# One load of wo behind the last V instead of sixteen small ones, in a decode kernel for a gated attention and MLP mix

## The chip, the cores and the metric

The kernel runs on one core of one Trainium2 chip. A core has TensorE (PE, whose weight loads are listed as PEld), VectorE (DVE), ScalarE (ACT), GpSimd (POOL) and SyncE (SP), 16 DMA engines that are fed here by SP's queue, an SBUF of 128 partitions and a PSUM of eight banks. The metric is the time of one execution on the device in microseconds (us), as the median of several runs; smaller is better.

## The reference

```python
def reference(A_x, A_k_cache, A_v_cache, A_wq, A_wo, B_x, B_w1, ..., gate_w):
    # B=2, Sq=1, D=1024, H=32, Sk=16384, Dh=128, F=3584, all bf16
    x = A_x
    g = sigmoid((x * gate_w).sum(-1, keepdims=True))
    q = (x @ wq) -> [B, H, 1, Dh]
    p = softmax(q . k_cache * Dh**-0.5)           # over 16384 keys
    a = (p . v_cache) -> [B, 1, H*Dh] @ wo
    h  = gelu(layernorm(x) @ w1)
    hs = shifted quarters of h (all zero for one token) @ w2
    x1 = x + hs
    b  = x1 + gelu(layernorm(x1) @ w3) @ w4
    return g * a + (1 - g) * b
```

K and V are 268 MB each. All weights together are 36 MB, of them wo 8 MB (4096 rows of 1024) and w4 7 MB.

## The kernel before

**Units.** A unit is one batch row `b` and a pair of heads `hp` (16 pairs). Its K is 8 MB and its V is 8 MB: 128 partitions with 64 KB each. For a unit the kernel transposes K in eight chunks on DVE (line 423), multiplies each with the query on PE (429) into a PSUM tile S, takes the softmax (`softmax_a`, `softmax_b`), multiplies the weights with V on PE (`pv`, 483), and finishes in `pv_end`: ACT scales the sums (496), 16 matmuls gather the four lanes of the two heads (504), and DVE multiplies by the gate into `oT` (512), which holds one pair of heads for both batch rows. After the second batch row, `project` multiplies `oT` with the pair's 256 rows of wo and adds the result into the PSUM tile `arow` (375). `arow` holds the whole output, 4 groups of 256 columns on different partitions, in one bank; it starts with the residual of the MLP (`mlp_residual`), collects all 16 pairs, then w4's product (`mlp_last`, 403), and is copied out in four pieces by `write_out`, two on DVE (524) and two on ACT (526).

**Memory.** A large SBUF tile `mem` is cut into five cells of 32 KB a partition. K of batch row 0 takes cells 0 and 1, K of batch row 1 takes cells 1 and 2, V takes cells 3 and 4. The order of the chunks (`halves`) is such that cell 1, which both K's use, is read first. A transfer can start when the cells that it writes have been read: K's next load waits for DVE's transposes, V's next load for PE's `pv`. wo's 512 KB for a pair go to a tile of their own, `wo_pair`, in rows of 4 KB.

**Order.** The first unit's work stands ahead of a loop of 15 rounds over `hp`. A round is `odd_rest(hp)` and `even_unit(hp + 1)`. The last unit stands in an arm inside the loop (`tc.If(i >= HP - 2)`), which every engine jumps over in all rounds but the last. In the rounds without it, each engine instead counts up the semaphores that the arm would have counted. `in_order` keeps each engine's instructions in the order in which they are written, SP's too. SP issues in a round: wo (367), K of batch row 0 (112), V (115), K of batch row 1 (112), V (115). A load that waits holds back those written behind it. The built program lets wo's load wait until PE has come past the arm of the round before, since the arm's `project` reads `wo_pair`.

**The last arm.** It loads the last V into cells 0 and 1 (`V_LAST`), wo's last 512 KB, and, when `pv(0)` has read cells 3 and 4, all of w4 into these in four pieces of 15, 7, 4 and 2 rows a partition. Then come `pv(1)`, `pv_end(1)`, `project`, `mlp_last` piece by piece, and `write_out`.

Of the kernel before, what the change touches and what calls it, by code (L numbers as in the profile page):

```python
# [10 lines left out]
FP32 = mybir.dt.float32  # L11
BF16 = mybir.dt.bfloat16
ACTF = mybir.ActivationFunctionType
ALU = mybir.AluOpType
# [9 lines left out]
def kernel(  # L24
# [15 lines left out]
    nc = tc.nc  # L40
    P = nc.NUM_PARTITIONS
    B, Sq, D = A_x.shape
    _, H, Sk, Dh = A_k_cache.shape
# [3 lines left out]
    KC = D // P  # L47
    FC = F // P
# [4 lines left out]
    HALF = P // 2  # L53
    NJ = 2 * Sk // P
# [4 lines left out]
    Q4 = 4  # L59
    QP = P // Q4  # L60
    CELL = NJ * Dh // 2
    G1 = D // Q4
# [3 lines left out]
    const = ctx.enter_context(tc.tile_pool(name="const", bufs=1))  # L66
# [3 lines left out]
    mlp = ctx.enter_context(tc.tile_pool(name="mlp", bufs=1))  # L70
    ops = ctx.enter_context(tc.tile_pool(name="ops", bufs=1, space=PSUM))
# [8 lines left out]
    def region(cell, elements, offset=0):  # L80
        at = cell * CELL + offset
        return mem[:, at : at + elements]
# [6 lines left out]
    def load_weight(W, cell, offset=0, pieces=None):  # L89
        K, N = W.shape  # L90
        dst = region(cell, K // P * N, offset)
        src = W.rearrange("(p r) n -> p (r n)", p=P)
        r = 0
        for n in pieces or (K // P,):
            at = slice(r * N, (r + n) * N)
            nc.sync.dma_start(out=dst[:, at], in_=src[:, at])
            r += n
        return dst.rearrange("p (r n) -> p r n", n=N)
# [5 lines left out]
    K_CELL = (0, 1)  # L104
    V_CELL = 3

    def cache_rows(cache, hp, b):
        two = cache[b, bass.ds(2 * hp, 2)]
        return two.rearrange("h s d -> (h s) d").rearrange("(p j) d -> p (j d)", p=P)

    def load_k(hp, b):
        nc.sync.dma_start(out=region(K_CELL[b], NJ * Dh), in_=cache_rows(A_k_cache, hp, b))  # L112

    def load_v(hp, b, cell=V_CELL):
        nc.sync.dma_start(out=region(cell, NJ * Dh), in_=cache_rows(A_v_cache, hp, b))
# [6 lines left out]
        out=ident_s[:], in0=ident_f[:], scalar1=-scale, scalar2=None, op0=ALU.mult  # L122
# [7 lines left out]
    mask4 = const.tile([P, Q4], BF16)  # L130
    nc.gpsimd.memset(mask4[:], 1.0)
    nc.gpsimd.affine_select(
        out=mask4[:], in_=mask4[:], compare_op=ALU.is_ge, fill=0.0,
# [3 lines left out]
        out=mask4[:], in_=mask4[:], compare_op=ALU.is_ge, fill=0.0,  # L137
# [11 lines left out]
        out=lmat[:].rearrange("p (g h k) -> p g h k", h=2, k=4),  # L149
        in_=hm2[:].unsqueeze(1).unsqueeze(3).to_broadcast([P, P // 8, 2, 4]),  # L150
# [3 lines left out]
    lane = const.tile([P, QP], FP32)  # L154
    nc.vector.tensor_reduce(
        out=lane[:],
        in_=ident_f[:].rearrange("p (c k) -> p k c", k=QP),
        axis=AX.X,
        op=ALU.add,
# [3 lines left out]
    for g in range(Q4):  # L163
        nc.vector.tensor_scalar(
            out=spread[:, g],
            in0=lane[:].unsqueeze(1).to_broadcast([P, Q4, QP]),
            scalar1=mask4[:, g : g + 1], scalar2=None, op0=ALU.mult,
        )

    oacc = [ops.tile([P, 4 * Dh], FP32, name=f"oacc{k}") for k in range(2)]  # L170
    arow = ops.tile([P, G1], FP32, name="arow")
    S_tiles = [ops.tile([P, GT * QP], FP32, name=f"S{k}") for k in range(2)]
    for t in (oacc[0], oacc[1], arow):
        nc.vector.memset(t[:], 0.0)

    WW = P + NG
# [2 lines left out]
    for k in range(2):  # L179
        t = const.tile([P, 4, WW], BF16, name=f"qw{k}")  # L180
# [37 lines left out]
    g_rep = const.tile([P, B], FP32)  # L218
# [141 lines left out]
        )  # L360


    wo_pair = const.tile([P, 2, D], BF16, name="wo_pair")

    def load_wo(hp):
        rows = A_wo[bass.ds(hp * 2 * Dh, 2 * Dh)]
        nc.sync.dma_start(  # L367
            out=wo_pair[:].rearrange("p t n -> p (t n)"),
            in_=rows.rearrange("(p t) n -> p (t n)", p=P),
        )  # L370

    def project():
        for t in range(2):
            for g in range(Q4):
                nc.tensor.matmul(
                    arow[QP * g : QP * g + B, :],
                    lhsT=oT[:, t, :],
                    rhs=wo_pair[:, t, g * G1 : (g + 1) * G1],
                    start=False,
                    stop=False,  # L380
                    skip_group_check=True,
                )

    def mlp_residual():
        x1g = mlp.tile([P, KC, B], FP32, name="x1g")
        nc.vector.tensor_tensor(
            out=x1g[:], in0=x1T[:], in1=spread_batch(omg, KC), op=ALU.mult
        )
        for r in range(KC):
            for g in range(Q4):  # L390
                nc.tensor.matmul(
                    arow[QP * g : QP * g + B, :].rearrange("b (i r) -> b r i", r=KC)[:, r, :],
                    lhsT=x1g[:, r, :],
                    rhs=ident_f[:, QP * g : QP * (g + 1)],
                    start=(r == 0),
                    stop=False,
                    skip_group_check=True,
                )

    def mlp_last(w4):  # L400
        for r in range(FC):
            for g in range(Q4):
                nc.tensor.matmul(  # L403
                    arow[QP * g : QP * g + B, :],
                    lhsT=h2T[:, r, :],
                    rhs=w4[:, r, g * G1 : (g + 1) * G1],
                    start=False,
                    stop=(r == FC - 1),
                    skip_group_check=True,
                )  # L410

# [77 lines left out]
            )  # L489


    oT = const.tile([P, 2, B], BF16, name="oT")

    def pv_end(b):
        osb = ppool.tile([P, 4 * Dh], FP32, name="osb")
        nc.scalar.activation(  # L496
            out=osb[:], in_=oacc[b][:], func=ACTF.Copy, scale=rinvs[b][:, 0:1]
        )
        lines = osb[:].rearrange("p (k d t) -> p k t d", k=4, t=2)
        ot = misc_psum([P, 2])  # L500
        for t in range(2):
            for k in range(4):
                for h in range(2):
                    nc.tensor.matmul(  # L504
                        ot[h * HALF : (h + 1) * HALF, t : t + 1],
                        lhsT=lines[:, k, t, :],
                        rhs=lane[:, k + 4 * h : k + 4 * h + 1],
                        start=(k == 0 and t == 0),
                        stop=(k == 3),
                        skip_group_check=True,  # L510
                    )
        nc.vector.tensor_scalar(  # L512
            out=oT[:, :, b], in0=ot[:], scalar1=g_rep[:, b : b + 1], scalar2=None, op0=ALU.mult
        )

    W4_PIECES = (15, 7, 4, 2)
    out_row = mlp.tile([B, D], BF16, name="out_row")

    def write_out():
        for g in range(Q4):  # L520
            at = out_row[:, g * G1 : (g + 1) * G1]
            row = arow[QP * g : QP * g + B, :]
            if g % 2 == 0:
                nc.vector.tensor_copy(out=at, in_=row)  # L524
            else:
                nc.scalar.activation(out=at, in_=row, func=ACTF.Copy)  # L526
        nc.sync.dma_start(out=out.rearrange("b s n -> (b s) n"), in_=out_row[:])
# [14 lines left out]
    softmax_b(0)  # L542
    score_first(0, 1)

    def odd_rest(hp):
        load_wo(hp)
        load_k(hp + 1, 0)
        score_second(1)
        softmax_a(1)
        pv(0)  # L550
        load_v(hp, 1)
        pv_end(0)
        softmax_b(1)

    def even_unit(hp):
        score_first(hp, 0)
        load_k(hp, 1)
        score_second(0)
        softmax_a(0)
        pv(1)  # L560
        load_v(hp, 0)
        pv_end(1)
        project()
        softmax_b(0)
        score_first(hp, 1)


    def last_unit(hp):
        V_LAST = 0
        load_v(hp, 1, V_LAST)  # L570
        load_wo(hp)
        score_second(1)
        softmax_a(1)
        pv(0)
        w4 = load_weight(B_w4, V_CELL, pieces=W4_PIECES)
        pv_end(0)
        softmax_b(1)
        pv(1, V_LAST)
        pv_end(1)
        project()  # L580
        mlp_last(w4)
        write_out()

    def in_order():

        last = {}
        for ins in nc.cur_bb.bb.instructions:
            if ins.engine in last:
                tc.add_manual_dep(
                    ins,  # L590
                    last[ins.engine].name,
                    mybir.DependencyInfo(
                        mybir.DependencyClass.NoSync, mybir.DependencyReason.DATA
                    ),
                    reason="in order",
                )
            last[ins.engine] = ins

    in_order()
    with tc.For_i(0, HP - 1, 1, iteration_sync="reg_based") as i:  # L600
        odd_rest(i)
        even_unit(i + 1)
        in_order()
        with tc.If(i >= HP - 2):  # L604
            last_unit(HP - 1)
            in_order()


# [28 lines left out]
```

## Time and profile before

| | |
|---|---|
| Time, median of 3 runs | 1337.62 us (1336.85 to 1338.44) |
| The profiled execution | 1337.09 us, of which 1334.9 us is the span of the profile |
| PE busy | 772.2 us (58%) |
| DVE busy | 652.4 us (49%) |
| ACT busy | 130.4 us (10%) |
| SP's DMA queue (q1) | 572.53 MB, 99.4% of the time of 16 DMA engines |
| Instruction queue (q8) | 8 packets of 16 KB |
| Granted TensorE clock, mean | 0.792 |

The page of a profile gives busy times by engine, the DMA queues, the chain of work that ended last, and groups of instructions with their count, total and mean duration and the idle time ahead of them. A timeline lists instructions in order: start, duration, engine, line, operation, tiles, and in brackets the idle time before and what ended it. "SPq" is an instruction of SP's sequencer, here the issue of a transfer. A window's row gives its bounds, length, the busy time of each engine, the TensorE clock, the share of the DMA engines and GB/s.

### The profile page before, as it was taken

How to read it: one execution, taken by the hardware profiler on the slowest of the kernel's cores; microseconds unless marked ns; L12 is line 12 of the kernel's file. 1: busy time of each engine (PE TensorE's matmuls, PEld its weight loads, DVE VectorE, ACT ScalarE, POOL GpSimd, SP SyncE). 2: the span in 40 equal slices, each digit the busy share in tenths (PEclk: the TensorE clock that was granted, in tenths of full speed). 3: DMA queues.
4: the chain of work that ended last, by engine and by line, in shares of the span. 5: the costliest groups of instructions: out<-in, count | busy, mean ns of one | idle time of the engine just before them, and what ended most of it. 6: DMA issues, size and time to landing. Idle time of an engine off the chain costs nothing. (4 is left out here: it accounts for less than half of the span.)

```text
span 1334.9 us, 14766 instructions
## 1 busy us (share of the span) xinstructions
PE 772.2 (58%) x5758; PEld 335.1 (25%) x5758; DVE 652.4 (49%) x510; ACT 130.4 (10%) x204; POOL 12.9 (1%) x47
## 2 busy tenths in 40 slices
PE   1554657455566545567555556655556765655763
PEld 1222223222222222222222222222222222222322
DVE  2454455444455544445553445555444555544550
ACT  0011101111110111110011111001111000111110
POOL 1000000000000000000000000000000000000000
PEclk9677878777888777788777788877778876778886
DMA  9999999999999999999999999999999999999997
GB/s 409 436 434 427 438 405 440 416 448 438 426 440 424 440 438 426 438 426 440 424 440 438 426 438 426 440 424 440 438 426 438 426 440 424 440 438 426 438 431 310
DMA packets 13101, 572.68 MB, mean 429 GB/s; under 512 B 1826, under 2 KB 1826, under 8 KB 4004
## 3 DMA queue, kind: packets, MB, share of 16 engines
q1 hardware_dynamic: 12676, 572.53, 99.4%
q8 instruction: 8, 0.13, 0.0%
q10 hardware_dynamic: 416, 0.01, 0.0%
q14 instruction: 1, 0.01, 0.0%
HBM read 572.53 MB, written 0.00 MB: 429 GB/s over the span
## 5 line engine op out<-in xcount | busy, mean ns | idle before, releaser
L429 PE MATMUL S<-KT,qw 128*128 128x512 bf16 x2048 | 554.7, 422 | 356.2 <-DVE KT L423 349.6
L423 DVE STREAM_TRANSPOSE KT<-mem 128x2048 f32<-128x2048 f32 x256 | 573.7, 2286 | 269.6 <-DMA mem<-in_A_k_cache_dram 95.6
L429 PEld LDWEIGHTS <-qw 128*128 128x128 bf16 x2048 | 220.8, 108 | 685.3 <-issue 512.7
L483 PE MATMUL oacc<-mem,pt 128*8 128x512 bf16 x2048 | 117.8, 383 | 8.2 <-DMA mem<-in_A_v_cache_dram 8.2
L454 ACT ACTIVATE Dm<-ident_s,m 128x128 f32<-128x128 f32 x32 | 12.9, 402 | 977.5 <-PE oacc L483 943.6
L467 ACT ACTIVATE pt<-St,nb 64x256 bf16<-64x256 f32 x64 | 89.7, 1402 | 79.4 <-DVE nb L465 78.5
L512 DVE TENSOR_SCALAR oT<-misc,g_rep 128x2 bf16<-128x2 f32 x32 | 7.1, 222 | 166.9 <-PE misc L504 166.9
L476 PE MATMUL misc<-rs,lmat 128*128 128x1 f32 x64 | 18.8, 362 | 106.9 <-ACT pt L467 61.2
L483 PEld LDWEIGHTS <-pt 128*8 128x8 bf16 x2048 | 47.3, 87 | 75.9 <-issue 23.8
L504 PE MATMUL misc<-lane,osb 128*64 128x1 f32 x1024 | 36.1, 199 | 45.3 <-ACT osb L496 45.3
L477 DVE RECIPROCAL rinv<-misc 128x1 f32<-128x1 f32 x32 | 5.4, 169 | 107.5 <-PE misc L476 104.2
L450 DVE STREAM_TRANSPOSE St<-S 128x512 f32<-128x512 f32 x32 | 22.9, 717 | 66.2 <-PE L483 64.2
L504 PEld LDWEIGHTS misc<-lane,osb 128*64 128x64 f32 x1024 | 33.8, 138 | 61.0 <-ACT osb L496 31.7
L476 PEld LDWEIGHTS misc<-rs,lmat 128*128 128x128 f32 x64 | 16.0, 311 | 114.0 <-ACT pt L467 64.7
L496 ACT ACTIVATE osb<-oacc,rinv 128x512 f32<-128x512 f32 x32 | 22.0, 687 | 88.7 <-PE oacc L483 88.7
L467 ACT ACTIVATION_READ_ACCUMULATOR pt<-St,nb 64x1 f32 x64 | 30.5, 477 | 0.0
L465 DVE TENSOR_REDUCE nb<-misc 64x1 f32<-64x64 f32 x64 | 14.2, 222 | 22.0 <-PE misc L460 21.0
L354 POOL TENSOR_TENSOR qw<-qdu,mask 128x16 bf16<-128x16 bf16 x32 | 8.4, 265 | 1181.3 <-PE L483 1109.2
L460 PE MATMUL misc<-Dm,ones_f 128*128 128x128 f32 x64 | 18.7, 380 | 0.0
L452 DVE TENSOR_REDUCE m<-St 128x1 f32<-128x256 f32 x32 | 13.4, 420 | 1.1
L460 PEld LDWEIGHTS misc<-Dm,ones_f 128*128 128x128 f32 x64 | 11.5, 226 | 5.3 <-issue 5.1
L203 DVE STREAM_TRANSPOSE turn<-wide 128x256 f32<-128x256 f32 (+2 forms) x5 | 3.4, 685 | 17.8 <-ACT wide L328 10.4
(80 smaller groups left out, 69.6 us busy)
## 6 DMA issues: line engine op xcount, KB each, us to landing
wo_pair<-in_A_wo_dram SPq DMA_DIRECT2D x16, 512.0 KB, 8.0
mem<-in_B_w_dram SPq DMA_DIRECT2D x1, 7168.0 KB, 31.7
mem<-in_B_w_dram SPq DMA_DIRECT2D x2, 2048.0 KB, 10.0
mem<-in_B_w_dram SPq DMA_DIRECT2D x1, 3840.0 KB, 26.7
mem<-in_B_w_dram SPq DMA_DIRECT2D x1, 1792.0 KB, 30.1
mem<-in_B_w_dram SPq DMA_DIRECT2D x1, 1024.0 KB, 32.1
mem<-in_A_k_cache_dram SPq DMA_DIRECT2D x32, 26.6
mem<-in_A_v_cache_dram SPq DMA_DIRECT2D x32, 31.7
```

The source lines that it names most:

```text
L423: nc.vector.transpose(out=kt[:], in_=Kc.rearrange("p j d -> p (j d)").bitcast(FP32))
L429: nc.tensor.matmul(S, lhsT=qw[b][:, v, NG - 1 - m : NG - 1 - m + P], rhs=ktb[:, half * GT : (half + 1) * GT, w, :, e], start=(first and n ...
L450: nc.vector.transpose(out=st[:].rearrange("p j r -> p (j r)"), in_=S[:])
L452: nc.vector.tensor_reduce(out=m[:], in_=st[:, :, 0:NG], axis=AX.XY, op=ALU.max)
L454: nc.scalar.activation(out=Dm[:], in_=ident_s[:], func=ACTF.Copy, scale=m[:, 0:1])
L460: nc.tensor.matmul(R_ps[:], lhsT=ones_f[:], rhs=Dm[:], start=True, stop=True)
L465: nc.vector.tensor_reduce(out=nb[rows], in_=R_ps[rows, rows], axis=AX.X, op=ALU.min)
L467: nc.scalar.activation(out=pts[b][rows, :, e, :].rearrange("p (m a) k -> p a k m", a=GT // 4), in_=st[rows, :, 0:NG].rearrange("p (a k) m ...
L476: nc.tensor.matmul(tot_ps[:], lhsT=lmat[:], rhs=rs[:], start=True, stop=True)
L483: nc.tensor.matmul(oacc[b][QP * q : QP * q + 8, :], lhsT=pts[b][:, g].rearrange("p h k -> p (h k)"), rhs=V[:, 4 * g : 4 * g + 4, :].rearra ...
L496: nc.scalar.activation(out=osb[:], in_=oacc[b][:], func=ACTF.Copy, scale=rinvs[b][:, 0:1])
L504: nc.tensor.matmul(ot[h * HALF : (h + 1) * HALF, t : t + 1], lhsT=lines[:, k, t, :], rhs=lane[:, k + 4 * h : k + 4 * h + 1], start=(k == 0 ...
```

## The change

wo is no longer loaded by pairs. The results of all pairs are kept in a tile `o_all` (two batch rows, 32 heads, fp32). `pv_end` writes the pair's two columns there, after four matmuls with a whole head's 128 columns as weights in place of 16. `project` leaves the loop. In the last arm, wo comes in one transfer of 64 KB a partition into V's cells behind `pv(0)`. `turn_heads` spreads the 32 heads over 128 columns with a mask (two DVE products), turns them with two matmuls, and copies the result to `o_turned`, in which partition p has the 32 numbers that belong to rows 32p to 32p + 31 of wo. `project` then takes 32 steps of four matmuls.

w4's first 15 rows a partition go to cell 2 (K's), in one transfer behind wo. The other three pieces go to cell 0 behind `pv(1)`. The output has two PSUM tiles, `arows[0]` for column groups 0 and 1, copied by DVE, and `arows[1]` for groups 2 and 3, copied by ACT. The loop's K loads are declared free of the last arm's instructions across rounds. In the built program, SP's round then starts with K's load, which waits for DVE's last transposes of the round before and for landings of K, and no longer stands behind a load that waits for PE.

```diff
-    wo_pair = const.tile([P, 2, D], BF16, name="wo_pair")
-    def load_wo(hp):
-        rows = A_wo[bass.ds(hp * 2 * Dh, 2 * Dh)]
-        nc.sync.dma_start(out=wo_pair[:]..., in_=rows.rearrange("(p t) n -> p (t n)", p=P))
-    def project():
-        for t in range(2):
+    def project(o_turned, wo):
+        for r in range(QP):
             for g in range(Q4):
                 nc.tensor.matmul(
-                    arow[QP * g : QP * g + B, :],
-                    lhsT=oT[:, t, :],
-                    rhs=wo_pair[:, t, g * G1 : (g + 1) * G1],
+                    arows[g // 2][QP * g : QP * g + B, :],
+                    lhsT=o_turned[:, r, :],
+                    rhs=wo[:, r, g * G1 : (g + 1) * G1],
...
-    def pv_end(b):
+    def pv_end(hp, b):
...
-        for t in range(2):
-            for k in range(4):
-                for h in range(2):
-                    nc.tensor.matmul(ot[h * HALF : (h + 1) * HALF, t : t + 1], lhsT=lines[:, k, t, :], ...)
+        for k in range(4):
+            nc.tensor.matmul(
+                ot[:], lhsT=osb[:, k * Dh : (k + 1) * Dh], rhs=lane[:, k : k + 5 : 4],
+                start=(k == 0), stop=(k == 3),
+            )
         nc.vector.tensor_scalar(
-            out=oT[:, :, b], in0=ot[:], scalar1=g_rep[:, b : b + 1], ...
+            out=o_all[:, b, bass.ds(2 * hp, 2)], in0=ot[:], scalar1=g_rep[:, b : b + 1], ...
+    def turn_heads():
+        apart = mlp.tile([P, B, H, Q4], BF16, name="apart")
+        for b in range(B):
+            nc.vector.tensor_tensor(out=apart[:, b], in0=o_all[:, b]..., in1=mask4[:]..., op=ALU.mult)
+        ps = misc_psum([P, B, QP])
+        for b in range(B):
+            nc.tensor.matmul(ps[:, b], lhsT=apart[:, b].rearrange("p h c -> p (h c)"), rhs=lane_b[:], ...)
+        t = mlp.tile([P, QP, B], BF16, name="o_turned")
+        nc.vector.tensor_copy(out=t[:], in_=ps[:].rearrange("p b r -> p r b"))
+        return t
+    def load_wo(cell):
+        dst = region(cell, QP * D)
+        nc.sync.dma_start(out=dst, in_=A_wo.rearrange("(p r) n -> p (r n)", p=P))
+        return dst.rearrange("p (r n) -> p r n", n=D)
...
     def write_out():
         for g in range(Q4):
             at = out_row[:, g * G1 : (g + 1) * G1]
-            row = arow[QP * g : QP * g + B, :]
-            if g % 2 == 0:
+            row = arows[g // 2][QP * g : QP * g + B, :]
+            if g < 2:
                 nc.vector.tensor_copy(out=at, in_=row)
             else:
                 nc.scalar.activation(out=at, in_=row, func=ACTF.Copy)
...
     def odd_rest(hp):
-        load_wo(hp)
-        load_k(hp + 1, 0)
+        loads.append(load_k(hp + 1, 0))
...
     def last_unit(hp):
         V_LAST = 0
         load_v(hp, 1, V_LAST)
-        load_wo(hp)
         score_second(1)
         softmax_a(1)
         pv(0)
-        w4 = load_weight(B_w4, V_CELL, pieces=W4_PIECES)
-        pv_end(0)
+        wo = load_wo(V_CELL)
+        w4_first = load_w4(2, 0, (W4_FIRST,))
+        pv_end(hp, 0)
         softmax_b(1)
         pv(1, V_LAST)
-        pv_end(1)
-        project()
-        mlp_last(w4)
+        w4_rest = load_w4(V_LAST, W4_FIRST, W4_REST)
+        pv_end(hp, 1)
+        project(turn_heads(), wo)
+        mlp_last(w4_first, 0)
+        mlp_last(w4_rest, W4_FIRST)
         write_out()
...
             last_unit(HP - 1)
             in_order()
+            for load in loads:
+                for ins in nc.cur_bb.bb.instructions:
+                    tc.declare_no_dep(load.ins, ins, across_iterations=True, reason="last round")
```

More of the change, by code (lines that the diff above doesn't have):

```diff
@@ L111, in load_k @@
     def load_k(hp, b):
-        nc.sync.dma_start(out=region(K_CELL[b], NJ * Dh), in_=cache_rows(A_k_cache, hp, b))
+        return nc.sync.dma_start(
+            out=region(K_CELL[b], NJ * Dh), in_=cache_rows(A_k_cache, hp, b)
+        )
     def load_v(hp, b, cell=V_CELL):
@@ L170 @@
     oacc = [ops.tile([P, 4 * Dh], FP32, name=f"oacc{k}") for k in range(2)]
-    arow = ops.tile([P, G1], FP32, name="arow")
+    arows = [ops.tile([P, G1], FP32, name=f"arow{k}") for k in range(2)]
     S_tiles = [ops.tile([P, GT * QP], FP32, name=f"S{k}") for k in range(2)]
-    for t in (oacc[0], oacc[1], arow):
+    for t in (*oacc, *arows):
         nc.vector.memset(t[:], 0.0)
@@ L360, in write_qw @@
         )
-    wo_pair = const.tile([P, 2, D], BF16, name="wo_pair")
-    def load_wo(hp):
-        rows = A_wo[bass.ds(hp * 2 * Dh, 2 * Dh)]
[L367 to L370, printed above, removed]
-    def project():
-        for t in range(2):
+    def project(o_turned, wo):
+        for r in range(QP):
             for g in range(Q4):
                 nc.tensor.matmul(
-                    arow[QP * g : QP * g + B, :],
-                    lhsT=oT[:, t, :],
-                    rhs=wo_pair[:, t, g * G1 : (g + 1) * G1],
+                    arows[g // 2][QP * g : QP * g + B, :],
+                    lhsT=o_turned[:, r, :],
+                    rhs=wo[:, r, g * G1 : (g + 1) * G1],
                     start=False,
@@ L391, in mlp_residual @@
                 nc.tensor.matmul(
-                    arow[QP * g : QP * g + B, :].rearrange("b (i r) -> b r i", r=KC)[:, r, :],
+                    arows[g // 2][QP * g : QP * g + B, :].rearrange("b (i r) -> b r i", r=KC)[:, r, :],
                     lhsT=x1g[:, r, :],
@@ L398, in mlp_residual, with mlp_last @@
                 )
-    def mlp_last(w4):
-        for r in range(FC):
+    def mlp_last(w4, first):
+        for r in range(w4.shape[1]):
             for g in range(Q4):
                 nc.tensor.matmul(
-                    arow[QP * g : QP * g + B, :],
-                    lhsT=h2T[:, r, :],
+                    arows[g // 2][QP * g : QP * g + B, :],
+                    lhsT=h2T[:, first + r, :],
                     rhs=w4[:, r, g * G1 : (g + 1) * G1],
                     start=False,
-                    stop=(r == FC - 1),
+                    stop=(first + r == FC - 1),
                     skip_group_check=True,
@@ L489, in pv @@
             )
-    oT = const.tile([P, 2, B], BF16, name="oT")
-    def pv_end(b):
+    o_all = const.tile([P, B, H], FP32, name="o_all")
+    def pv_end(hp, b):
         osb = ppool.tile([P, 4 * Dh], FP32, name="osb")
@@ L498, in pv_end @@
         )
-        lines = osb[:].rearrange("p (k d t) -> p k t d", k=4, t=2)
         ot = misc_psum([P, 2])
-        for t in range(2):
-            for k in range(4):
-                for h in range(2):
[L504 to L511, printed above, removed]
+        for k in range(4):
+            nc.tensor.matmul(
+                ot[:], lhsT=osb[:, k * Dh : (k + 1) * Dh], rhs=lane[:, k : k + 5 : 4],
+                start=(k == 0), stop=(k == 3),
+            )
@@ L512, in pv_end @@
         nc.vector.tensor_scalar(
-            out=oT[:, :, b], in0=ot[:], scalar1=g_rep[:, b : b + 1], scalar2=None, op0=ALU.mult
-        )
-    W4_PIECES = (15, 7, 4, 2)
+            out=o_all[:, b, bass.ds(2 * hp, 2)], in0=ot[:], scalar1=g_rep[:, b : b + 1],
+            scalar2=None, op0=ALU.mult,
+        )
+    lane_b = const.tile([P, QP], BF16)
+    nc.vector.tensor_copy(out=lane_b[:], in_=lane[:])
+    def turn_heads():
+        apart = mlp.tile([P, B, H, Q4], BF16, name="apart")
+        for b in range(B):
+            nc.vector.tensor_tensor(
+                out=apart[:, b],
+                in0=o_all[:, b].unsqueeze(2).to_broadcast([P, H, Q4]),
+                in1=mask4[:].unsqueeze(1).to_broadcast([P, H, Q4]),
+                op=ALU.mult,
+            )
+        ps = misc_psum([P, B, QP])
+        for b in range(B):
+            nc.tensor.matmul(
+                ps[:, b], lhsT=apart[:, b].rearrange("p h c -> p (h c)"), rhs=lane_b[:],
+                start=True, stop=True,
+            )
+        t = mlp.tile([P, QP, B], BF16, name="o_turned")
+        nc.vector.tensor_copy(out=t[:], in_=ps[:].rearrange("p b r -> p r b"))
+        return t
@@ new lines, in load_wo, with load_w4 @@
+    def load_wo(cell):
+        dst = region(cell, QP * D)
+        nc.sync.dma_start(out=dst, in_=A_wo.rearrange("(p r) n -> p (r n)", p=P))
+        return dst.rearrange("p (r n) -> p r n", n=D)
+    W4_FIRST = 15
+    W4_REST = (7, 4, 2)
+    def load_w4(cell, r, pieces):
+        dst = region(cell, (FC - r) * D)
+        src = B_w4.rearrange("(p r) n -> p (r n)", p=P)
+        at = 0
+        for n in pieces:
+            nc.sync.dma_start(
+                out=dst[:, at * D : (at + n) * D], in_=src[:, (r + at) * D : (r + at + n) * D]
+            )
+            at += n
+        return dst[:, : at * D].rearrange("p (r n) -> p r n", n=D)
@@ L543 @@
     score_first(0, 1)
+    loads = []
     def odd_rest(hp):
-        load_wo(hp)
-        load_k(hp + 1, 0)
+        loads.append(load_k(hp + 1, 0))
         score_second(1)
@@ L556, in even_unit @@
         score_first(hp, 0)
-        load_k(hp, 1)
+        loads.append(load_k(hp, 1))
         score_second(0)
@@ L561, in even_unit @@
         load_v(hp, 0)
-        pv_end(1)
-        project()
+        pv_end(hp - 1, 1)
         softmax_b(0)
@@ L574, in last_unit @@
         pv(0)
-        w4 = load_weight(B_w4, V_CELL, pieces=W4_PIECES)
-        pv_end(0)
+        wo = load_wo(V_CELL)
+        w4_first = load_w4(2, 0, (W4_FIRST,))
+        pv_end(hp, 0)
         softmax_b(1)
         pv(1, V_LAST)
-        pv_end(1)
-        project()
-        mlp_last(w4)
+        w4_rest = load_w4(V_LAST, W4_FIRST, W4_REST)
[3 more added lines that the diff above has]
+        mlp_last(w4_rest, W4_FIRST)
         write_out()
@@ L606 @@
             in_order()
+            for load in loads:
+                for ins in nc.cur_bb.bb.instructions:
+                    tc.declare_no_dep(
+                        load.ins, ins, across_iterations=True, reason="last round"
+                    )
 _INS = ['A_x', 'A_k_cache', 'A_v_cache', 'A_wq', 'A_wo', 'B_x', 'B_w1', 'B_w2', 'B_w3', 'B_w4', 'gate_w']
```

## The prediction

> **What bounds the kernel now.** I read the page first: busy shares, then the DMA queues.
>
> ```profile
> ## 3 DMA queue, kind: packets, MB, share of 16 engines
> q1 hardware_dynamic: 12676, 572.53, 99.4%
> q8 instruction: 8, 0.13, 0.0%
> ```
>
> SP's queue q1 carries all loads and keeps the 16 DMA engines busy for 99.4% of the span; PE has 58%, DVE 49%. So a change pays only if it shortens the transfers, fills a hole in q1, or shortens what follows the last landing. 0.6% of 1334.9 us is 8 us: a head of about 2, the end after the last landing (1329.16 to 1334.9), and little else. Second view, the timeline of SP in a late round:
>
> ```profile
> 1126.45 0.34 SPq L367 DMA_DIRECT2D wo_pair<-in_A_wo_dram  x1
> 1127.21 0.33 SPq L112 DMA_DIRECT2D mem<-in_A_k_cache_dram  x1
> ...
> 1205.14 0.33 SPq L367 DMA_DIRECT2D wo_pair<-in_A_wo_dram  x1
> 1205.89 0.33 SPq L112 DMA_DIRECT2D mem<-in_A_k_cache_dram  x1
> ```
>
> A round takes 78.69 us. The page gives a K load 26.6 us from issue to landing and a V load 31.7. Each transfer also leaves 16 completion marks in the trace, one per DMA engine. V's first mark is at 1211.03, wo's at 1212.31, K's at 1231.66: 1.28 us for wo's 512 KB, 19.35 for 8 MB. Four times 19.35 plus 1.28 is 78.68, the round. So K's 26.6 us hold 7 us of queueing: late rounds never starve. Third view, the branch over the last arm (L604), the timeline at the end of the loop's first round, and the DMA share there:
>
> ```profile
> L604 PEldq COMPARE_BRANCH  x16: 87/227/6551, 179.1 to 1329.2; - x16
> ```
> ```profile
> 185.92 0.34 SPq L367 DMA_DIRECT2D wo_pair<-in_A_wo_dram  x1
> 186.19 4.50 DVE L423 STREAM_TRANSPOSE KT<-mem 128x2048 f32<-128x2048 f32 x2 [7.13 <-PEq L604]
> 186.69 0.33 SPq L112 DMA_DIRECT2D mem<-in_A_k_cache_dram  x1
> ```
> ```profile
> 185.00:186.00 1.00, 0.00 (x0) 0.00 (x0) 0.00 (x0) 0.00 (x0) 0.00 (x0) 0.50 0.15 66
> 186.00:187.00 1.00, 0.00 (x0) 0.00 (x0) 0.81 (x1) 0.00 (x0) 0.00 (x0) 0.50 0.07 25
> ```
>
> PE's first jump over the arm took 6551 ns, with a code fetch (a q8 packet) inside it; the other rounds show some 230. The wo load waited for PE to pass, K's load stood behind it, and q1 ran dry: next to last column, 0.15 and 0.07 (packets counted where they start). By the marks, V ends at 186.09 on the earliest engine and 187.92 on the latest, the next K at 208.32 and 209.46. The earliest lost 208.32 - 186.09 - 1.28 - 19.35 = 1.60 us, the latest 0.91. Fourth view, the chain that ended last, from the last landing:
>
> ```profile
> 1329.16 0.04 issue
> 1329.20 0.81 PE arow L403 x8
> 1330.00 0.02 issue
> 1330.03 0.42 DVE out_row L524
> 1330.45 0.02 issue
> 1330.47 0.38 ACT out_row L526
> 1330.85 0.02 issue
> 1330.88 0.43 DVE out_row L524
> 1331.31 0.02 issue
> 1331.33 0.38 ACT out_row L526
> ```
>
> DVE and ACT take turns on one tile: 1.68 us in series.
>
> **wo in one load.** Sixteen loads at 1.28 us are 20.48 us of q1; one of 8 MB, by the K row, 19.35. Gain 1.1. Between them: 0 if wo's rows come at the old pace, 1.6 if the sixteen cost 163 ns a packet (the 4 KB packets' mean). The marks already hold overlaps, so 1.1. By the Trainium skill (DMA: Bandwidth & Descriptors, "Anatomy of one DMA"), a load on GpSimd's path costs about 2.0 us plus bytes/436e3; taken for SP's queue, an estimate from that page is 15 fixed costs saved, 30 us, and a sum of 32. The trace disagrees: a wo load adds 1.28 us here.
>
> **K's load freed.** wo's load waited for PE's pass over the arm; K's next load now heads SP's round and, in the built program, waits for DVE's last transposes of the round before and K landings. In late rounds it moves from 1205.89 to about 1203.1 (end of those transposes): worth 0, 7 us of queue cover it. In the loop's second round it moves from 186.69 to about 179, before V drains. The hole goes: 1.60 us on the earliest engine. Not all stays. Each code fetch sets one DMA engine back some 1.3 to 1.5 us; the hole let the laggards catch up (spread of the marks 1.84 us before, 0.9 in late rounds). Two fetches in the last arm (1289, 1301) bring it to 1.66 at the end. Unequalised, 1.84 remains, or about 2.0 if a fetch hits an engine already 0.5 behind: 0.2 to 0.4 back. If it hits one already at 1.84, 1.6 back. I take 1.3 net, with 0 and 1.6 as ends. What is late next is V's load behind pv(0): 202.70, about 201.4 without the first wo, while K's data last until 204.2; with 0.9 us from issue to flow, 1.9 us remain.
>
> **Heads kept.** Per pv_end 32 PE passes (1.13 us) become four fp32 products of 128x128. L460's two take 0.49 to 0.80, so 1.0 to 1.6; DVE still writes one 128x2 (222 ns), at an address from a register. The loop's eight project matmuls (0.60) leave. All lie under the 7 us of queue: 0; with that cover gone, half a microsecond a round either way. Prologue: another memset (272 ns) and a small copy (some 0.2), hidden behind loads queued to 51 us: 0, else 0.5 once.
>
> **The last arm.** wo waits for pv(0) (w4's issue at 1294.50 in before) and its turn comes when V_LAST drains at 1309.06: 14.6 us of cover. w4's first piece stands behind it and waits for DVE's last transposes, which are over. The other pieces wait for pv(1) on cell 0, until some 5.8 us after V_LAST lands; behind them on SP stands only the output. Ahead in q1 are then still 19.35 + 9.1 - 5.8 = 22 us: 0. Turning the heads (two DVE products, nearest row 0.22 us at 56 columns, so 0.2 to 0.6 each; two matmuls; one copy) takes about 2 us, against 11 before wo lands. project's 128 matmuls at L403's 3.29/60 us are 7.0; w4's first piece lands 9.1 after wo. At 80 ns they would be 10.2, and PE would still catch up within the 8 us of the last pieces: 0.
>
> **Two banks.** DVE does two copies while ACT does two: 0.42 + 0.43 instead of 1.68. Gain 0.8; 0 if the engines still take turns.
>
> **Sum.** 1.1 + 1.3 + 0.8 = 3.2 us. The profiled execution took 1337.09 (span 1334.9 and 2.2 around it), so 1333.9; the median of the three runs is 0.53 above it, so 1334.4.
>
> **Rivals.** (a) *The hole's gain is given back.* The slowest engine sets the end, and it lost less in the hole; or the first jump takes over 1.9 us longer with K's packets queued too, and the hole moves to V's load. For: by the second round the marks show seven engines set back. Against: each was set back once, and the two late fetches hit engines that were not behind. Then 1.1 + 0.8 = 1.9: 1335.7, within 0.2%.
> (b) *Slower: PE's code no longer stays loaded.* The arm grows (128 project matmuls for 8), and PE jumps over it every round. If the jump and the way back each cost 6.55 us, a round stalls 12.6 more. V's load, issued at 1221.64, has until K drains at 1231.66, less 0.9: 9.1 us. From there on each microsecond is lost per round: 3.5 times 13 rounds is 45 us, near 1380. A single stall would hide. Against: after 183 us no fetch until 1289, and the loop's own code shrinks (no project, shorter pv_end). The Trainium skill (Runtime: NRT & Kernel Launch, "Instruction fetch mechanics") says a taken branch out of a two-page window forces a fetch; the rounds at 227 ns disagree. The same section's 2048 instructions for PE would hold it.
> (c) *Each transfer pays a start.* If the 15 removed loads had each cost the shortest wo landing, 4.2 us, less 1.28, 44 us would go: 1293. The 99.4% leave no room. This would be the Trainium skill's 2.0 us at work.
> (d) *The change does not do what it says:* K's load still waits and the copies still alternate. Then 1.1: 1336.5, no change.
>
> **Chances.** Forecast (gain 2.7 to 3.8) 0.53; (a) 0.26; (b) 0.05; (c) 0.02; (d) 0.06; slower by something not named here, 0.08. The range takes the forecast's bounds and (a) and (d), with the runs' spread of 0.8 to either side: 1332.8 to 1337.0. A measurement of this kernel tells about 0.2% (2.7 us) from no change. Faster by more: the forecast and (c), 0.55; within it: (a) and (d), 0.32; slower: (b) and the unnamed, 0.13.
>
> **What would show it.** Right: wo's single load takes 19.3 to 19.4 us between its neighbours' marks; K's second-round load is issued near 179 and no slice falls under 0.9 there; rounds of 77.4 us; the last landing near 1326.8; DVE's and ACT's output copies overlap; q8 still 8 or 9 packets. Wrong: a hole at V's load near 205, marks over 2.5 us apart at the end, L604-like branches of several us in every round, or project running past the landing of w4's last piece.

## The result and the profile after

The changed kernel takes 1333.74 us (median of 10 runs, 1333.26 to 1335.7), the kernel before 1337.97 in the runs beside it (10 runs, 1336.85 to 1339.28). The ratio is 0.9968 with a 95% interval of 0.9959 to 0.9977: 4.2 us less, where the prediction said 3.2. The profiled execution took 1333.32 us with a span of 1331.1, and is 3.77 us shorter than the profiled one of before. The granted clock is 0.795 (0.792 before). Below, "before" and "after" by themselves are the two kernels.

The DMA queues on the page after (queue, packets, MB, share of 16 engines' span):

```profile
q1 hardware_dynamic: 10516, 572.53, 99.5%
q8 instruction: 8, 0.13, 0.0%
```

The same bytes go in 2160 packets fewer, the queue is as full as before, and the count of code fetches did not move. SP's timeline in a late round of after:

```profile
1184.35 0.33 SPq L112 DMA_DIRECT2D mem<-in_A_k_cache_dram  x1
1201.55 0.33 SPq L117 DMA_DIRECT2D mem<-in_A_v_cache_dram  x1
```

K's load now heads the round alone. By the completion marks a round takes 77.41 us, four times 19.35 (the first, from 184.74 to 262.24, takes 77.50). PE's branch over the arm (ns: min/median/max), and the timeline of after where the hole was:

```profile
L636 PEldq COMPARE_BRANCH  x16: 87/232/6403, 178.0 to 1326.3; - x16
```
```profile
177.95 1.90 PE L423 MATMUL S<-KT,qw 128*128 128x512 bf16 x8 [0.30 <-DVEq L636]
178.12 0.34 SPq L112 DMA_DIRECT2D mem<-in_A_k_cache_dram  x1
184.77 2.31 DVE L417 STREAM_TRANSPOSE KT<-mem 128x2048 f32<-128x2048 f32 x1 [6.87 <-PEq L636]
```

PE's slow first jump is still there (6403 ns), and DVE still waits for it: 6.87 us. But K's load was issued at 178.12, when that jump had just begun (178.0) and 6.3 us before it ended, so the queue has its data. The marks show V on the earliest engine at 184.74 and K at 204.08, 19.34 later: no hole. The windows there read so (last columns: DMA share, GB/s):

```profile
184.00:185.00 1.00, 0.00 (x0) 0.00 (x0) 0.23 (x1) 0.00 (x0) 0.00 (x0) 0.50 1.22 524
185.00:186.00 1.00, 0.00 (x0) 0.10 (x1) 1.00 (x1) 0.00 (x0) 0.00 (x0) 0.50 0.61 262
186.00:187.00 1.00, 0.00 (x0) 0.00 (x0) 1.00 (x1) 0.00 (x0) 0.00 (x0) 0.50 1.06 459
```

The 0.61 is no hole: a packet of 64 KB lasts 2.42 us here and is counted whole where it starts, so single slices swing between 0.6 and 1.2. The last part of the timeline:

```profile
1298.16 0.22 DVE L524 CAST o_turned<-misc 128x64 bf16<-128x64 f32 x1 [0.28 <-PE misc L519]
1309.13 6.39 PE L369 MATMUL arow<-mem,o_turned 128*2 128x256 bf16 x128 [11.01 <-DMA mem<-in_A_wo_dram]
1318.23 2.21 PE L397 MATMUL arow<-mem,h2T 128*2 128x256 bf16 x60 [2.71 <-DMA mem<-in_B_w_dram]
...
1326.94 0.86 DVE L554 CAST out_row<-arow 2x256 bf16<-2x256 f32 x2 [28.56 <-PE arow L397]
1327.06 0.78 ACT L556 ACTIVATE out_row<-arow 2x256 bf16<-2x256 f32 x2 [30.95 <-PE arow L397]
1327.89 0.33 SPq L557 DMA_DIRECT2D out_dram<-out_row  x1
```

The turned heads are ready at 1298.38, 10.7 us before wo has landed. `project` takes 6.39 us and then PE waits 2.71 for w4's first piece, so the end is set by landings alone. The output copies lie beside each other. The chain that ended last, of after:

```profile
1293.03 33.17 DMA mem<-in_B_w_dram
1326.19 0.04 issue
1326.23 0.81 PE arow L397 x7
1327.04 0.02 issue
1327.06 0.07 ACT out_row L556
```

The last landing is at 1326.19 (1329.16 before), and the output's transfer is issued 1.70 us later (2.57 before). So the 3.77 us split into 2.97 in front of the last landing and 0.87 behind it, less 0.07 from there to the end.

### The profile page after: what moved, and what is told of

The parts are those of the page before. It is cut to its first block, busy times and chain, and to the rows that moved or that the text cites. A ratio compares the mean times of both kernels' runs of the same rounds, so it can differ in the third digit from the quotient of the medians.

```text
span 1331.1 us, 13114 instructions
## 1 busy us (share of the span) xinstructions
PE 762.2 (57%) x4992; PEld 330.9 (25%) x4992; DVE 652.8 (49%) x515; ACT 130.4 (10%) x204; POOL 13.2 (1%) x47
## 5 line engine op out<-in xcount | busy, mean ns | idle before, releaser
L499 DVE TENSOR_SCALAR o_all<-misc,g_rep 128x2 f32 (+1 forms) x32 | 7.0, 220 | 161.9 <-PE misc L495 161.9
L495 PE MATMUL misc<-lane,osb 128*128 128x2 f32 x256 | 33.3, 252 | 45.4 <-ACT osb L490 45.4
L495 PEld LDWEIGHTS misc<-lane,osb 128*128 128x128 f32 x256 | 31.0, 191 | 61.1 <-ACT osb L490 31.7
L454 PE MATMUL misc<-Dm,ones_f 128*128 128x128 f32 x64 | 15.4, 323 | 0.0
L369 PE MATMUL arow<-mem,o_turned 128*2 128x256 bf16 x128 | 6.4, 364 | 11.0 <-DMA mem<-in_A_wo_dram 11.0
```

The source lines that it names most:

```text
L454: nc.tensor.matmul(R_ps[:], lhsT=ones_f[:], rhs=Dm[:], start=True, stop=True)
L495: nc.tensor.matmul(ot[:], lhsT=osb[:, k * Dh : (k + 1) * Dh], rhs=lane[:, k : k + 5 : 4], start=(k == 0), stop=(k == 3),)
```

## The experiments

Each edit is given against the kernel that it starts from. Differences of medians are beside the kernel before of the same runs (1337.74 us, 33 runs, for the first four; 1338.03, 18 runs, for the last three) or beside the changed kernel's 1333.74.

**1. Only the order of SP's round, on the kernel before.** wo stays in sixteen small loads, but behind K's, and both K loads of a round are declared free as in the change.

```diff
...
     def odd_rest(hp):
+        loads.append(load_k(hp + 1, 0))
         load_wo(hp)
-        load_k(hp + 1, 0)
...
-        load_k(hp, 1)
+        loads.append(load_k(hp, 1))
...
+            for load in loads:
+                for ins in nc.cur_bb.bb.instructions:
+                    tc.declare_no_dep(load.ins, ins, across_iterations=True, reason="last round")
```

> The kernel before, with two edits only: in a round, wo's small load is issued behind K's, and the loop's K loads are declared free of the last arm. The sixteen small loads of wo, the project matmuls in the loop and the single output tile stay. Theory 1 (the gain has three parts, and the hole in the loop's second round is the largest): K's load in the second round is issued near 179 us instead of 186.69, the DMA share does not drop there, the last landing comes 1.6 to 1.9 us before 1329.16, and the time falls by about 1.8 us, to a ratio near 0.9987. Theory 2 (the hole's gain is given back, because the slowest DMA engine lost less in it and stays behind): the hole closes too, but the last landing moves by less than 0.5 us, ratio 0.9996 to 1.0.

Measured: 1335.81 us (ratio 0.9985, 0.9976 to 0.9994), 1.93 less than before. SP's timeline in the loop's second round, and the last landing in the chain that ended last:

```profile
179.26 0.34 SPq L112 DMA_DIRECT2D mem<-in_A_k_cache_dram  x1
185.80 0.33 SPq L367 DMA_DIRECT2D wo_pair<-in_A_wo_dram  x1
202.79 0.33 SPq L115 DMA_DIRECT2D mem<-in_A_v_cache_dram  x1
```
```profile
1327.17 0.04 issue
```

wo's load still waits for PE until 185.80, but K's data cover it: V's first mark 185.92, K's 205.29, wo's 206.57, nothing lost. The marks are 1.70 us apart at the end (1.66 in before) and the last landing, at 1327.17, comes 1.99 us earlier. So closing the hole pays by itself, and is not given back. It pays 0.4 us more than the 1.60 that the prediction measured; the section on the prediction comes back to this.

**2. Only the two banks, on the kernel before.**

```diff
...
-    arow = ops.tile([P, G1], FP32, name="arow")
+    arows = [ops.tile([P, G1], FP32, name=f"arow{k}") for k in range(2)]
...
-            row = arow[QP * g : QP * g + B, :]
-            if g % 2 == 0:
+            row = arows[g // 2][QP * g : QP * g + B, :]
+            if g < 2:
```

> The kernel before, with the output in two PSUM tiles, the first copied by DVE, the second by ACT, and nothing else changed. Theory 1: the last landing stays at 1329.1 to 1329.2 us in the profile (or moves only by what the runs scatter), DVE's two copies lie beside ACT's two, and the output's transfer is issued 1.7 us after the last landing instead of 2.57: 0.85 us less, ratio 0.9994. Rival: the two engines still take turns, or the copies get longer beside each other: 0 to 0.3 us less.

Measured: 1336.68 us (ratio 0.999, 0.9981 to 1.0), 1.06 less; the interval just reaches no change. The copies overlap in the timeline, and the output is issued 1.69 us after the last landing (1331.72; in before 2.57 us):

```profile
1332.46 0.86 DVE L524 CAST out_row<-arow 2x256 bf16<-2x256 f32 x2 [10.97 <-PE arow L403]
1332.58 0.78 ACT L526 ACTIVATE out_row<-arow 2x256 bf16<-2x256 f32 x2 [12.57 <-PE arow L403]
1333.41 0.34 SPq L527 DMA_DIRECT2D out_dram<-out_row  x1
```

The profiled execution was this kernel's longest, 1338.77, and shows why. Its windows in the loop's second round, and SP's first load there:

```profile
184.00:186.00 2.00, 0.00 (x0) 0.00 (x0) 0.00 (x0) 0.00 (x0) 0.00 (x0) 1.00 0.49 205
186.00:188.00 2.00, 0.00 (x0) 0.00 (x0) 0.00 (x0) 0.00 (x0) 0.00 (x0) 0.85 0.00 0
```
```profile
188.40 0.34 SPq L367 DMA_DIRECT2D wo_pair<-in_A_wo_dram  x1
```

PE came to its first jump at 180.1 us (179.1 in the profiled execution of before) and took 8.03 us over it instead of 6.55; the code packet came at 185.81 (183.31). So wo's load left 2.5 us later and the queue stood empty: added up from the marks as in the prediction, 4.30 us were lost on the earliest engine and 2.45 on the latest. The last landing came 2.56 us later than in before, where no shift was expected. Of the two holes on record the prediction measured the smaller. In these two executions the hole's size followed when PE reached the jump and how long its code took to come.

**3. The changed kernel with wo in short rows.** One transfer of the same 8 MB, but sixteen stretches of 4 KB a partition in place of one of 64 KB. The rows of wo then meet other heads' numbers.

```diff
-        nc.sync.dma_start(out=dst, in_=A_wo.rearrange("(p r) n -> p (r n)", p=P))
+        nc.sync.dma_start(
+            out=dst.rearrange("p (i n) -> p i n", n=2 * D),
+            in_=A_wo.rearrange("(i p t) n -> p i (t n)", p=P, t=2),
+        )
```

> The kernel after the change, with wo still in one transfer behind the last V, but read in sixteen stretches of 4 KB per partition instead of one of 64 KB. wo's rows then stand in another order than the heads, so the products belong to other heads; the work is the same. Theory 1 (a short row costs time in the DMA engines, not the number of transfers): between the first completion marks of V and wo lie 20.3 to 20.6 us instead of 19.36, the last landing comes 1.0 to 1.2 us later than 1326.19, the time is 1334.8 to 1335.0. Theory 2 (what the change saved was a cost per transfer): 19.4 us between the marks, and no difference to the kernel after.

Measured: 1334.89 us (ratio 0.9979, 0.997 to 0.9988), 1.15 more than the changed kernel. The queue on the page, with 1920 packets more than in after:

```profile
q1 hardware_dynamic: 12436, 572.53, 99.5%
```

From V_LAST's first mark (1287.95) to wo's (1308.40) it is 20.45 us, where the long rows take 19.36. The packets of 4 KB take 164 ns on average, 16 of them 2.62 us, a packet of 64 KB 2.42. So the gain of wo's load comes from long rows, and a transfer by itself costs next to nothing: one transfer in short rows is as slow as sixteen (20.48). The last landing (1327.87) came 1.68 us later than in after, more than the 1.0 to 1.2 expected: the marks end 2.33 us apart (1.80 in after), since a late code fetch hit an engine that was already behind. It moved one of the 16 marks, from 0.83 us behind the first to 2.36.

**4. The changed kernel without K's declaration.**

```diff
-            for load in loads:
-                for ins in nc.cur_bb.bb.instructions:
-                    tc.declare_no_dep(load.ins, ins, across_iterations=True, reason="last round")
```

> The kernel after the change, without the declaration that frees the loop's K loads from the last arm; all else stays. In the built program K's first load of a round then waits for PE again. Theory 1: in late rounds K's load is issued some 2 us later than in the kernel after and nothing else moves; in the second round it is issued at 184.5 to 185 us instead of 178.12, while V drains at 184.74 on the earliest DMA engine, so that a hole of 0.8 to 1.1 us returns there; the last landing comes 0.5 to 1.0 us later than 1326.19, ratio to the kernel before 0.9974 to 0.9978. Theory 2 (the earlier K loads give a gain in every round): 15 rounds of 2 us, 1360 us or more. Theory 3 (the hole is worth nothing): as the kernel after, 0.9968.

Measured: 1335.57 us (ratio 0.9987, 0.9978 to 0.9996), 1.83 more than the changed kernel. The last landing came 2.04 us later (1328.23). The first theory had said 0.5 to 1.0 for it: right in kind, too small. The timeline there, and the window:

```profile
184.79 0.34 SPq L112 DMA_DIRECT2D mem<-in_A_k_cache_dram  x1
184.86 4.50 DVE L417 STREAM_TRANSPOSE KT<-mem 128x2048 f32<-128x2048 f32 x2 [7.03 <-PEq L636]
```
```profile
184.00:185.00 1.00, 0.00 (x0) 0.00 (x0) 0.14 (x1) 0.00 (x0) 0.00 (x0) 0.50 0.01 0
```

K's load waits for PE again and leaves at 184.79, the very moment when V has landed on the earliest engine (184.81). Still that engine loses 206.07 - 184.81 - 19.35 = 1.91 us, the latest 0.97. The trace's packets show both parts of a restart: the first of K's starts 0.97 us after the issue, and the first packet on each engine takes 2.6 to 3.3 us instead of 2.42. I had counted the first part alone. The late rounds take 77.4 us, as in the changed kernel.

**5. The changed kernel with a longer arm.** 350 tiny matmuls (700 instructions of PE) between `turn_heads` and `project`.

```diff
-        project(turn_heads(), wo)
+        o_turned = turn_heads()
+        idle = misc_psum([2, 2])
+        for _ in range(350):
+            nc.tensor.matmul(idle[:], lhsT=lane_b[:, 0:2], rhs=lane_b[:, 0:2], start=True, stop=True)
+        project(o_turned, wo)
```

> The kernel after the change, with 350 more matmuls (two columns by two, in bf16, results unused) in the last arm between turn_heads and project: 700 PE instructions more to jump over in each of the 14 other rounds, executed once while PE waits for wo. It tests the rival that the longer arm makes PE fetch code in every round. Theory 1 (PE keeps the blocks of code that it has used, whatever lies between them): the branch over the arm takes 6 to 7 us once and 220 to 240 ns in the 13 other rounds, rounds stay at 77.41 us; only the end has 2 or 3 more code fetches, each setting one DMA engine back by 1.3 to 1.5 us, so 11 or 12 instruction packets in all and an end 0 to 3 us later, up to 1337. Theory 2 (the rival: jump target and loop head push each other out): two fetches and 12 us of PE stall in each round against 9 us of queue, so 14 rounds with 3 us or more lost, 1375 us or more, and 30 or more instruction packets.

Measured: 1340.52 us (ratio 1.0017, 1.0008 to 1.0027), 6.8 more than the changed kernel: over what was expected. PE's branch, and the last arm:

```profile
L642 PEldq COMPARE_BRANCH  x16: 87/232/6672, 178.0 to 1332.4; - x16
```
```profile
1298.93 19.40 PE L614 MATMUL misc<-lane_b 128*2 128x2 bf16 x350
...
1318.23 7.89 PE L369 MATMUL arow<-mem,o_turned 128*2 128x256 bf16 x128
1325.91 6.93 PE L397 MATMUL arow<-mem,h2T 128*2 128x256 bf16 x112
```

For the question it was run for, the answer is clear: one slow jump and then 232 ns, rounds of 77.4 us. An arm of some 700 instructions more is jumped over at no price. The time went elsewhere. The tiny matmuls took 55 ns each, 19.4 us in all, past wo's landing, so `project` began 9 us late and PE ran past the last landing (1327.71). The arm also fetched more code (13 packets on q8 instead of 8; 11 or 12 were expected), and the marks ended 3.05 us apart. The expectation had the tiny matmuls fit into PE's wait for wo, and they did not.

**6. The changed kernel with a smaller last piece of w4.**

```diff
-    W4_REST = (7, 4, 2)
+    W4_REST = (7, 5, 1)
```

> The kernel after the change, with w4's last pieces of 7, 5 and 1 rows instead of 7, 4 and 2, so that four matmuls instead of eight follow the last landing. All theories: the last landing as in the kernel after within 0.3 us; from there to the first copy of the output 0.5 to 0.7 us instead of 0.81; time 0.1 to 0.3 us less than the kernel after, which the timing can't tell from none, only the chain that ended last can. If DVE's first copy waits for something else, no difference there either.

Measured: 1334.1 us (ratio 0.9974, 0.9963 to 0.9984; 8 runs), no gain. Its chain:

```profile
1325.60 0.04 issue
1325.64 1.77 PE arow L397 x24
1327.40 0.02 issue
1327.43 0.07 ACT out_row L556
```

The chain does not start at the last landing (1326.22) but at that of the piece before, 1325.60: its 20 matmuls and the last 4 take 1.77 us. ACT's first copy begins 1.2 us after the last landing, against 0.87 with the split 7, 4, 2, so the expected 0.5 to 0.7 did not come: the larger piece before holds PE up.

**7. The changed kernel with an eighth transfer in the arm.**

```diff
-    W4_REST = (7, 4, 2)
+    W4_REST = (7, 3, 2, 1)
```

> The kernel after the change, with w4's last pieces of 7, 3, 2 and 1 rows: one transfer more in the last arm, eight instead of seven. The eighth shares its semaphore with V's second load of a round, so in every round SP, passing the arm by, waits until that V has landed before it can issue K's load. This takes away the queue's cover of K's load (some 7 us). Theory 1 (the cover is what makes late K loads free, and a queue that runs dry costs the time from the landing to the next flow): K's load is issued just after V's last mark in each round, each round gets a hole of 1 us or more on the slowest DMA engine, rounds of 78.4 to 79 us instead of 77.41, 15 to 25 us in all, 1348 to 1358 us, and the spread of the marks shrinks below 1 us. Theory 2 (the transfer time alone sets the rounds, holes are given back): under 3 us more than the kernel after.

Measured: 1387.35 us (ratio 1.037, 1.0355 to 1.0386; 4 runs), 54 more than the changed kernel, where 15 to 25 were expected. A late round in the timeline:

```profile
1242.26 4.50 DVE L417 STREAM_TRANSPOSE KT<-mem 128x2048 f32<-128x2048 f32 x2 [9.39 <-SPq L636]
1243.13 0.33 SPq L112 DMA_DIRECT2D mem<-in_A_k_cache_dram  x1
```

The arm's eighth transfer is now the output's. Its completion marks stand in the trace on the semaphore of V's second load; in the changed kernel, with seven, the output's marks stand on that of K's second load, which lands one load earlier. In every round SP comes past the arm only after V has landed (last mark 1241.89), DVE waits for SP, and K's load leaves into an empty queue. From V's first mark (1241.44) to K's (1264.33) it is 22.89 us, a hole of 3.5 us: 1.69 from the mark to K's issue, and 1.85 for the restart, as in experiment 4. A round takes 80.93 to 81.5 us, the first 82.4, and q1's share falls to 96.3%. The 14 rounds from V's mark at 184.98 to that at 1322.45 take 1137.47 us where those of the changed kernel take 1083.79, which is 53.7 of the 54 us. That the shared semaphore is what SP waits for is read from the program and fits the trace; no run with the transfer on a semaphore of its own was made.

**Together.** Alone, the parts save 1.93 (order), 1.06 (banks) and 1.15 (long rows), in sum 4.1 us; the change as a whole saves 4.2. Each part carries an interval of some 1.2 us to either side, so that the sum comes out this close is partly luck.

## Why the prediction was right, and which term was too small

**What bounds the kernel** held: the end is set by landings, PE waits for w4 to the last, and nothing that the change put on PE, DVE or ACT shows in the time.

**wo in one load** came out as summed: 19.36 us between neighbours' marks, against sixteen at 1.28, 1.1 us less. Experiment 1 gives the price of a small load over the whole loop: from K's mark in the second round to V_LAST's, 56 loads of 8 MB take 1101.75 us there, with 14 loads of wo among them, and 1083.80 in after, without. That makes 1.28 apiece.

**K's load freed** was the term that was too small: 1.3, where the runs show about 1.8. It took 0.2 to 0.4 us off the hole's 1.60 for the lag of single engines. The hole closed in full, and the marks' last spread rose only from 1.66 to 1.80 us, so 0.14 was given back. And the prediction put nothing for what follows a hole: in before the same 56 loads with 13 of wo take 1100.74 us, 0.3 more than 1083.80 and 13 x 1.28. The difference lies in the first rounds behind the hole, where loads of 8 MB step by up to 19.46 us (V's mark at 227.70, K's at 247.16) before they settle at 19.35. Experiment 4 shows 0.3 too (1084.07), experiment 1, without a hole, none. Why the steps are longer there is open. With it, 1.60 + 0.3 - 0.14 is about 1.8, near what experiments 1 and 4 measure (1.93 and 1.83).

The hole of one profiled execution was also taken for the hole of the kernel, while experiment 2 shows a larger one. The span of the profiled execution of before, 1334.9 us, is 0.5 shorter than the median span (1335.4) of the 33 runs of before beside experiments 1 to 4, and the profiled one of after has the median span of its kernel (1331.1). This can be the reason for the medians' 4.2 against the profiled executions' 3.77. That it is the hole that varies in those 33 runs is not shown, since only one of before was profiled.

The lag itself behaves as described. In after the marks of late rounds are 1.86 us apart; in before they are 0.9 apart after the hole. The Trainium skill (DMA: Bandwidth & Descriptors, "Queues, rings and completion order") says that each DMA engine takes turns between the queues by whole packets; the trace agrees as far as it goes: a code packet of 16 KB takes 1.07 us, and the first fetch of the last arm of after moves one of the 16 marks, from 0.21 us behind the first to 1.72, and leaves the others. That the queues take turns is not seen in it.

**V's load as the next late thing** came closer than worked out. It left at 201.44, as predicted (201.4), 2.64 us before K's earliest mark (204.08). Of the 1.9 us said to remain, nothing did: V's earliest mark came 19.45 after K's, so 0.1 was lost. In experiments 3 and 6 V's load left 2.71 and 2.78 us ahead of K's mark and at most 0.02 was lost; in experiment 5 it left 2.28 ahead and lost 0.27. The step of the prediction that failed here is the 0.9 us from issue to flow: it is the first part of a restart alone, as in experiment 4. So a hole was about to open at V's load, as rival (a) had it; it is worth a tenth of a microsecond.

**Two banks**: 0.87, said 0.8. **The terms at nothing** show nothing in the time: `pv_end`'s four products are 1.05 us (said 1.0 to 1.6), turning the heads 1.1 (said 2), `project` 6.39 (said 7.0), each with its cover left over.

The sum by the measured sizes is 1.1 + 1.8 + 0.87 = 3.8 us, against 3.77 in the profiled executions. The gain of the medians, 4.2 us, lies above the forecast's own bounds of 2.7 to 3.8; the time lies inside the range, which is wider by the runs' spread and by the rivals. That range was added up with a slip: 1337.6 less 3.8 and 0.8 is 1333.0, not 1332.8, and (d)'s 1336.5 and 0.8 make 1337.3, not 1337.0. The measured 1333.74 lies in both.

**The rivals.** (a) falls by experiments 1 and 4: freeing K alone saves 1.93 us, taking it away costs 1.83. Nor did the first jump take longer with K's packets queued (6.40 us against 6.55). (b) falls by the branch line of after and by experiment 5. The two-page rule that the prediction weighed (the Trainium skill, Runtime: NRT & Kernel Launch, "Instruction fetch mechanics") does not fit these traces either: between PE's first jump and the last arm, from 183 to 1277 us in after, no code packet comes, although PE jumps over the arm in every round. (c) falls by experiment 3, (d) by SP's timeline and the copies in after. One sign was put badly: "no slice under 0.9" was not met, as slices of 1 us are shorter than a packet; marks are the right view for it.

## What to carry to other kernels

When one queue of transfers is 99% full, look for the few places where it runs dry, and put a load that waits for nothing new ahead of one that waits for a busy engine. Count a restart of the queue with both its parts, and look at a hole in more than one execution before it is priced. In this queue the length of a transfer's rows mattered more than the number of transfers, and one transfer more in a rarely taken arm can put a wait into every round.

## What the runs showed of the hardware

- A queue that has run dry costs more than its late issue: the first packet starts 0.97 us after the issue, and the first packets of 64 KB take 2.6 to 3.3 us instead of 2.42, 1.9 us in all on the earliest engine (experiment 4).
- A code packet comes late into a full queue: 4.0 us after PE's jump began in after (178.0 and 182.01), 4.2 in before (179.1 and 183.31), 5.7 in experiment 2 (180.1 and 185.81). That it waits there behind data packets is likely, but not shown. One fetch sets one of the 16 engines back by about 1.5 us, and the spread of the marks then stays until the queue has a hole: 1.9 us held over a thousand microseconds in after.
- PE's jump over an arm costs 6.4 to 6.7 us the first time (8.0 in experiment 2) and some 230 ns from then on, for the arm of the change and for one 700 instructions longer.
- 8 MB take 20.45 us of the queue in rows of 4 KB and 19.36 in rows of 64 KB, both in one transfer (experiment 3 and after).
